# The last 24 key steps of attention in threes, with a third place for scores and six adds on another engine

## The chip, the core and the metric

The program runs on one core of a Trainium2 chip. The core has TensorE (PE in the profile, with its weight loads as PEld), VectorE (DVE), ScalarE (ACT), GpSimd (POOL) and SyncE (SP, which here only starts DMAs). Each engine executes its own instructions in the order in which the program issued them and waits on semaphores for the others. Matmul results go to PSUM, which has room for eight tiles of 128 x 512 float32; everything else lives in SBUF or in DRAM, and sixteen DMA engines move data. The metric is device microseconds from the first to the last instruction of one execution; the time of a kernel is the median over its runs.

## The reference

Two blocks, run twice: attention with 32 heads of 32 columns over 2048 tokens of 1024 columns, and a feed-forward (SwiGLU, 3584 wide) on only the eight tokens that score highest.

```
x = A_x
x = x + A(layernorm(x));  x = x + B(layernorm(x))
x = x + A(layernorm(x));  x = x + B(layernorm(x))

A: q, k, v = split(x @ wqkv);  p = softmax(q k^T / sqrt(32));  return (p v) @ wo
B: r = x @ w_r;  idx = the 8 largest r;  xs = x[idx]
   y = (silu(xs @ w_gate) * (xs @ w_up)) @ w_down;  y = y * sigmoid(r[idx])
   return x with y added in the rows idx
```
All is float32. The kernel multiplies float32 as sums of rounded high and low parts where it needs the precision.

## The kernel before, in words

`layer(n, ...)` is one attention with its feed-forward; layer 1 is a generator whose first stages are interleaved with the end of layer 0, and it takes over layer 0's feed-forward. Scheduling is manual: each engine runs its instructions in program order, and the framework adds the semaphores and hands out buffers of a pool as earlier tiles in them come free.

**Attention.** The work is cut into 32 units: a group of four heads (8 groups) by a block of 512 queries (4 blocks). A unit has 16 key steps of 128 keys. The loop over `s` goes through all 512 steps; for step `s`:

- `scores` (L698) makes two half steps of scores, two heads each, with four matmuls per half into a PSUM tile `pre` of 128 x 1024. There are two such tiles.
- ACT takes the exponential of each half (L1099) into the step's tile `P`, 128 x 2048 float32. There are nine `P` buffers (`PB`).
- `pv_step` (L1025) multiplies an earlier step's `P` by the values into one PSUM tile `pv`; in the last 25 steps it is two steps behind.
- `pre_mm` (L688) multiplies queries and keys once more, 25 steps ahead (`LEAD`), and DVE takes the row maxima of it (L696) from the three PSUM tiles `st`. So in the last 25 steps there is no such work, and DVE is nearly free.
- The denominators: `emit` (by the table `EVENTS`, made by `unit_events`) adds the 16 `P` tiles of a unit into `acc`. Ten tiles are joined in pairs by DMAs that add in SBUF (`merge`, L1038, issued by POOL), and eight adds of 128 x 2048 go to POOL (`acc_add`, L1035, at the steps of `ADDED`). The last unit has no merges: its twelve adds are on DVE. `sum_mm` (L1045) multiplies `acc` and two or three `P` tiles left over by ones on PE, and ACT copies the result (L1055). For the second-to-last unit this comes in step 22, counted from that unit's start.

A `P` buffer is free again when its P times V and its add, merge or sum are done.

PSUM is full: `pre` 2 x 2 places, `pv` 1, `st` 3. After the loop and the last `sum_mm` comes the output projection (L1238), tile by tile of 128 tokens, with the residual, the layer norm's statistics and the router's logits on DVE (L1243 to L1273).

**The end of layer 1.** The last two tiles (L1303) are handled apart: `row_sums` (L1312, L1315), `logits`, `normed`, and between them `first_rows` and `last_rows`, which pick the candidates of the router and gather their rows. Then `finish` runs 49 steps of the feed-forward: for each of two halves eight gate steps, eight up steps (L531, accumulated in the PSUM tile `pv`) and a transpose (L548), then 14 down steps (L563) and the final scatter (L579). The gate's result is made into its silu by ACT (L538, L539), DVE (L540, L541) and POOL (L542), and DVE multiplies it with up (L544). Weights are loaded by SP as buffers come free. In between, `choose` ranks the candidates, and `back(1)` and `back(0)` move rows of the output into their places: each gathers rows (POOL, L216), loads eight rows (ACT's queue, L382) and scatters both (POOL, L220). POOL waits in its queue for each of these transfers before it starts the next that depends on it.

## Time and profile before

| | us |
|---|---|
| median of 3 runs (4557.66 to 4558.62) | 4558.31 |
| the profiled execution | 4557.8 |
| its span, first to last instruction | 4556.0 |
| PE busy in the span | 4506.4 |
| from the scores of step 8 of the second-to-last unit to the output projection, layer 0 | 64.94 |
| the same in layer 1 | 64.97 |
| PE busy in these two stretches | 62.39 and 62.38 |
| from 4440 to the end: length, and PE busy in it | 116.00, 90.89 |

A profile's row gives the time at which a group of like instructions starts (us from the start of the span), its length, engine and line, the operation with the tiles that it writes and reads, the count, and in brackets how long the engine was idle before it and what ended that. Engines that wait often belong to a chain: the view of the chain goes back from the last instruction to whatever released it. A busy PE is not PE at its best, since matmuls overlap and their ends are modelled; waits inside a stretch are better seen in the distance from start to start. Rows of stretches give the busy time of each engine in a window, TensorE's granted clock, the DMA engines' share and GB/s.

### The profile page before, as it was taken

To read this page: it belongs to the slowest core of one execution; us is meant where nothing else is said; L and a number is where in the kernel's file an instruction comes from. 1 tells how busy PE (TensorE), PEld (TensorE's weight loads), DVE (VectorE), ACT (ScalarE), POOL (GpSimd) and SP (SyncE) were. 2 spreads that over 40 slices of the span, in tenths; PEclk is the share of its full clock that TensorE was granted. 3 is DMA by queue.
4 is the path that set the end of the run, shared out by engine and by line. 5 is a ranking of instruction groups with operands and counts; after the bars stand their busy time and mean duration, and the time that the engine had idled before them with its cause. 6 is when DMAs were issued, how large, how long until landed. Compare 5 with 4: busy or idle time off the path is not lost.

```text
span 4556.0 us, 73559 instructions
## 1 busy us (share of the span) xinstructions
PE 4506.4 (99%) x29241; PEld 2686.4 (59%) x29241; DVE 3150.2 (69%) x4963; ACT 2428.5 (53%) x2574; POOL 3231.7 (71%) x1251
## 2 busy tenths in 40 slices
PE   9999999999999999999999999999999999999997
PEld 7888745555555555548877786555555555555583
DVE  2211588888888888876522225888888888888663
ACT  3322267767676767670222222767777676767510
POOL 4444378989898889855633343888989898989452
PEclk9999999999999999999999999999999999999998
DMA  6757477777777768758698774877777777777598
GB/s 206 210 171 207 130 170 154 171 156 160 167 163 158 172 145 180 168 122 242 183 318 279 252 207 122 175 153 166 164 152 174 157 160 167 164 158 175 140 277 322
DMA packets 329719, 833.62 MB, mean 183 GB/s; under 512 B 43996, under 2 KB 160732, under 8 KB 280206
## 3 DMA queue, kind: packets, MB, share of 16 engines
q1 hardware_dynamic: 275454, 476.43, 35.4%
q0 software_dynamic: 45248, 325.67, 35.3%
q10 hardware_dynamic: 8672, 26.81, 2.2%
q8 instruction: 230, 3.77, 0.3%
q14 instruction: 115, 0.94, 0.1%
HBM read 384.34 MB, written 119.47 MB: 111 GB/s over the span
## 4 chain that ended last, share of the span: by engine, by line
PE 94%; DMA 2%; POOL 1%; issue 1%; DVE 1%; ACT 0%; ACTq 0%; POOLq 0%; SPq 0%; DVEq 0%
PE pv L1025 22%; PE pre L703 21%; PE st L821 17%; PE st L688 16%; PE pre L821 6%; PE pre L1238 5%; PE st L1045 4%; POOL acc L1035 1%; PE pv L531 1%; PE pre L688 1%; PE pv L821 0%; PE pre L790 0%; DMA ord<-rd 0%; PE st L571 0%; PE pre L1303 0%
## 5 line engine op out<-in xcount | busy, mean ns | idle before, releaser
L696 DVE TENSOR_REDUCE nm<-st 128x1 f32<-128x512 f32 x3916 | 2434.0, 684 | 376.1 <-PE st L688 370.1
L1099 ACT ACTIVATE P<-pre 128x1024 f32<-128x1024 f32 x2048 | 1985.9, 1022 | 723.3 <-PE pre L703 521.4
L1035 POOL TENSOR_TENSOR acc<-acc,P 128x2048 f32<-128x2048 f32 x434 | 2103.9, 4848 | 86.2 <-DMA P<-P 75.4
L703 PE MATMUL pre<-q,ks 64*128 64x512 f32 (+1 forms) x8192 | 1142.4, 396 | 4.3 <-ACT P L1099 4.3
L1025 PE MATMUL pv<-P,v 128*32 128x512 f32 x8192 | 1092.8, 606 | 4.8 <-DMA v<-vd 4.8
L688 PEld LDWEIGHTS st<-ks,q 64*128 64x128 f32 x3916 | 547.0, 184 | 907.4 <-DVE nm L696 764.9
L688 PE MATMUL st<-ks,q 64*128 64x512 f32 x3916 | 985.9, 471 | 0.5
L703 PEld LDWEIGHTS pre<-q,ks 64*128 64x128 f32 (+1 forms) x8192 | 776.1, 187 | 186.0 <-ACT P L1099 57.4
L1038 POOL DMA_DIRECT2D P<-P x310 | 296.8, 957 | 260.0 <-PE st L688 189.3
L836 DVE TENSOR_TENSOR lo<-st,hi 128x512 fp32r<-128x512 f32 x128 | 88.4, 692 | 528.4 <-ACT hi L835 505.2
L756 POOL TENSOR_TENSOR ohl<-wraw,ord 128x2048 fp32r<-128x2048 f32 (+1 forms) x54 | 222.5, 4124 | 308.1 <-ACT ord L751 299.5
L756 POOL TENSOR_TENSOR wl<-wraw,wh 128x2048 fp32r<-128x2048 f32 (+1 forms) x54 | 222.4, 4122 | 303.7 <-ACT wh L755 284.9
L835 ACT CAST hi<-st 128x512 fp32r<-128x512 f32 x128 | 75.2, 587 | 496.5 <-PE st L821 493.3
L1025 PEld LDWEIGHTS pv<-P,v 128*32 128x32 f32 x8192 | 162.5, 108 | 261.3 <-issue 253.6
L1035 POOL TENSOR_TENSOR acc<-P 128x2048 f32<-128x2048 f32 x62 | 294.0, 4742 | 11.0 <-ACT P L1099 11.0
L1238 PE MATMUL pre<-woh,ohl 128*128 128x512 f32 x960 | 223.2, 390 | 0.0
L1238 PEld LDWEIGHTS pre<-woh,ohl 128*128 128x128 f32 x960 | 180.0, 188 | 39.6 <-ACT ohl L1170 1.7
L821 PE MATMUL st<-xh,wh 128*128 128x512 f32 x512 | 201.4, 393 | 0.0
L821 PE MATMUL st<-xh,wl 128*128 128x512 f32 x512 | 199.6, 390 | 0.0
L821 PE MATMUL st<-xl,wh 128*128 128x512 f32 x512 | 199.5, 390 | 0.0
L151 POOL TENSOR_TENSOR rs<-mv,eps_c 128x1 f32<-128x1 f32 x64 | 29.3, 457 | 232.2 <-DVE mv L149 232.2
L1170 ACT CAST ohl<-ord 128x1024 fp32r<-128x1024 f32 x32 | 33.6, 1052 | 269.9 <-DVE ord L1161 115.7
(384 smaller groups left out, 3995.7 us busy)
## 6 DMA issues: line engine op xcount, KB each, us to landing
P<-P POOLq DMA_DIRECT2D x310, 1024.0 KB, 8.8
wraw<-in_A_wqkv_dram SPq DMA_DIRECT2D x96, 1024.0 KB
q<-qh SPq DMA_DIRECT2D x256, 128.0 KB
ks<-kh SPq DMA_DIRECT2D x112, 256.0 KB
fw<-in_B_w_down_dram SPq DMA_DIRECT2D x17, 1024.0 KB
vd<-vn SPq DMA_DIRECT2D x32, 512.0 KB
qh<-hi SPq DMA_DIRECT2D x64, 256.0 KB
ql<-lo SPq DMA_DIRECT2D x64, 256.0 KB
```

The source lines that it names most:

```text
L688: pe.matmul(ps[b], Q[u][rows, i, 0, qt * 128:(qt + 1) * 128], KS[(u // QC) % 2][rows, i, 0, j * 512:(j + 1) * 512], start=True, stop=True, ...
L696: dve.tensor_reduce(NM[u][:, j, 2 * i + b:2 * i + b + 1, qt], ps[b], axis=AX.X, op=OP.max, negate=True)
L703: pe.matmul(p[:, b * 512:(b + 1) * 512], KS[(u // QC) % 2][rows, i, slot, kt * 128:(kt + 1) * 128], Q[u][rows, i, slot, :], start=(slot == ...
L756: pool.tensor_tensor(wl[:, sl], raw[:, sl], wh[:, sl].bitcast(F32), op=OP.subtract)
L821: pe.matmul(p, *pair(a, l, r), start=(a == 0 and k == 0), stop=(a == KD - 1 and k == 2))
L836: dve.tensor_tensor(lo, p, hi.bitcast(F32), op=OP.subtract)
L1025: pe.matmul(PV[u][32 * h:32 * h + 32, :], V[g][:, kt, 32 * h:32 * h + 32], P[s][:, h, :], start=(kt == 0), stop=(kt == NT - 1), tile_posit ...
L1035: (dve if on_dve else pool).tensor_tensor(o, a, P[u * NT + k].rearrange("p h c -> p (h c)"), op=OP.add)
L1038: pool.dma_start(P[u * NT + a], P[u * NT + b], accum_op=OP.add)
L1045: pe.matmul(p[32 * h:32 * h + 32, :], ones32, a[:, h, :], start=(i == 0), stop=(i == len(parts) - 1), tile_position=(0, 32 * h))
L1099: act.activation(P[s][:, 2 * i:2 * i + 2, :].rearrange("p h c -> p (h c)"), p, AF.Exp, scale=SCALE)
L1238: pe.matmul(p[:, bl], l[:, a, :], r[a][:, bl], start=(k == 0 and a == 0), stop=(k == 2 and a == KD - 1))
```

## The change

It has seven edits.

1. The three `st` places move into a PSUM pool of their own, `banks`. For the last 24 steps it is closed and opened again with one `st` and one `third` tile of 128 x 1024, which is a third place for scores; after the attention it is set back.
2. Those 24 steps run in threes: the six halves of three steps use `pre`, `pre`, `third` in turn. After the third half comes the P times V that is due, with the bookkeeping (`rest_of_step`: the events, DMA issues) of the first step; after the sixth come the next two P times V and the bookkeeping of the other two steps.
3. In the second-to-last unit the six adds of steps 9, 12, 14, 15, 16 and 20 go to DVE. Two adds (steps 5 and 6) and the merges stay on POOL.
4. In layer 1's feed-forward the up product accumulates in an `st` tile, not in `pv`.
5. `back` becomes a generator with a pause between the gather and load and the scatters; `finish` runs the parts after steps 3 and 8 (`back(1)`, before after step 2) and 17 and 25 (`back(0)`, before after step 9).
6. In layer 1's output projection the scaling of the last tile's attention result (`scale_o(NT - 1)`, L1161) moves on DVE from before the normalisation and the logits of tile 12 to behind them.
7. In `row_sums` the statistics of the first half come ahead of the step of `last_rows`, no longer behind it.

```diff
-def unit_events(last):
-    if last:
+ON_DVE = 9
+def unit_events(left):
+    if left == 0:
...
-    ev += [(at, "end", 1, "add", (k, FIRST if at == ADDED[0][0] else None, False)) for at, k in ADDED]
+    ev += [(at, "end", 1, "add", (k, FIRST if at == ADDED[0][0] else None, left == 1 and at >= ON_DVE)) for at, k in ADDED]
...
+    def share_banks(wide):
+        for st, _ in [banks["now"]] if banks else []:
+            st.close()
+        st = ExitStack()
+        banks["now"] = st, st.enter_context(tc.tile_pool(name="banks", bufs=1, space=PSUM))
+        banks["wide"] = wide
...
     def ps_st():
-        return psum.tile([128, 512], F32, name="st", bufs=3)
+        return banks["now"][1].tile([128, 512], F32, name="st", bufs=1 if banks["wide"] else 3)
...
             self.gather(rows, perm["ab"][:, 1:2], self.dst)
             act.dma_start(last, self.dst[end - 8:end, :])
+            yield
             self.scatter(perm["ab"][:, 0:1], rows, self.dst)
             self.scatter(perm["routed"], last, self.dst)
+            yield
...
-                    self.acc = ps_pv()
+                    self.acc = ps_st() if self.n and k == "u" else ps_pv()
...
+            parts = {0: choice, 2: choice, 3: backs[1], 8: backs[1], 17: backs[0], 25: backs[0]}
...
-                if i in (0, 2):
-                    next(choice)
-                if i == 9:
-                    self.back(0)
+                if i in parts:
+                    next(parts[i])
...
-        def scores(u, kt, i):
-            p = ps_pre()
+        def scores(u, kt, i, third=False):
+            p = banks["now"][1].tile([128, 1024], F32, name="third") if third else ps_pre()
...
+            threes = NS - LEAD + 1
+            for s in [*range(threes), *range(threes, NS, 3), *range(NS, NS + 14)]:
+                if threes <= s < NS:
+                    if s == threes:
+                        share_banks(True)
+                    for k in range(6):
+                        half_step(s + k // 2, k % 2, k % 3 == 2)
+                        if k == 2:
+                            pv_step(s - 2)
+                            rest_of_step(s)
+                    for k in (1, 2):
+                        pv_step(s - 2 + k)
+                    for k in (1, 2):
+                        rest_of_step(s + k)
+                    continue
...
-                if n and t == NT - 4:
-                    scale_o(NT - 1)
...
                 dve.scalar_tensor_tensor(waste, xn, 1.0, wrb, op0=OP.mult, op1=OP.mult, accum_out=rcols[:, t:t + 1])
+                if n and t == NT - 4:
+                    scale_o(NT - 1)
...
                     dve.tensor_tensor(o, p[i][h], o, op=OP.add)
+                    dve.bn_stats(st[:, h, :], o)
                     if between and h == 0:
                         next(between)
-                    dve.bn_stats(st[:, h, :], o)
```

More of the change, by code (lines that the diff above doesn't have):

```diff
@@ L599, in finish @@
         def finish(self):
-            choice = self.choose()
+            choice, backs = self.choose(), [self.back(i) for i in range(2)]
+            parts = {0: choice, 2: choice, 3: backs[1], 8: backs[1], 17: backs[0], 25: backs[0]}
             for i in range(len(self.steps)):
@@ L1080, in emit @@
                     if 0 <= v < NU:
-                        todo += [(kt + NT * back, pri, fn, args, v) for (k, pos, pri, fn, args) in EVENTS[v == NU - 1]
+                        todo += [(kt + NT * back, pri, fn, args, v) for (k, pos, pri, fn, args) in EVENTS[min(NU - 1 - v, 2)]
                                  if k == kt + NT * back and pos == where]
@@ L1089, in layer, with half_step, rest_of_step @@
             wop = None
[L1090 removed]
+            def half_step(s, i, third=False):
+                if i == 0:
+                    P[s] = aw.tile([128, 4, 512], F32, name="P", bufs=PB)
+                p = scores(*divmod(s, NT), i, third)
+                act.activation(P[s][:, 2 * i:2 * i + 2, :].rearrange("p h c -> p (h c)"), p, AF.Exp, scale=SCALE)
+            shared = {}
+            def rest_of_step(s):
                 u, kt = divmod(s, NT)
[L1092 to L1093 removed]
                 pr = pre_rows[s + LEAD] if s + LEAD < NS else None
[L1095 to L1104 removed]
                 emit(s, "mid")
@@ L1129, in layer @@
                     f(*args)
+            threes = NS - LEAD + 1
+            assert (NS - threes) % 3 == 0
+            for s in [*range(threes), *range(threes, NS, 3), *range(NS, NS + 14)]:
[12 more added lines that the diff above has]
+                    continue
+                pr = pre_rows[s + LEAD] if s + LEAD < NS else None
+                if pr:
+                    pre_mm(*pr, 0, False)
+                for i in range(2 if s < NS else 0):
+                    half_step(s, i)
+                if pr:
+                    pre_mm(*pr, 1, False)
+                t = s - 1 if s < NS - LEAD else s - 2
+                if s != NS - LEAD and 0 <= t < NS:
+                    pv_step(t)
+                rest_of_step(s)
+            wor, WOR, last_sum = shared["wor"], shared["WOR"], shared["sum"]
         if not prev:
```

36 lines of the change are left out of this document (13 added, 23 removed).

## The prediction

> **What bounds the kernel now.** I read the page's busy line and chain first, then the chain in order of time and the engines' timelines over the attention tail, and then the end of the kernel.
>
> ```profile
> PE 4506.4 (99%) x29241; PEld 2686.4 (59%) x29241; DVE 3150.2 (69%) x4963; ACT 2428.5 (53%) x2574; POOL 3231.7 (71%) x1251
> ...
> L1099 ACT ACTIVATE P<-pre 128x1024 f32<-128x1024 f32 x2048 | 1985.9, 1022 | 723.3 <-PE pre L703 521.4
> ...
> P<-P POOLq DMA_DIRECT2D x310, 1024.0 KB, 8.8
> ```
> ```profile
> 2001.00 6.48 POOL acc L1035
> ...
> 2028.04 2.71 PE pv L1025 x24
> 2030.76 3.43 PE st L1045 x32
> 2034.19 33.27 PE pre L1238 x144
> ...
> 4287.05 153.03 PE pre L1238 x672
> ```
> TensorE is nearly always busy, so only places where it waits can give time back. The second fence (the chain in order of time, both layers) shows one: a POOL add on the chain inside the last 24 key steps. I count key steps from the start of a layer's second-to-last unit, so these are 8 to 31, and T0 is the start of the scores of step 8.
>
> ```profile
> 1957.01 1.10 PE L703 MATMUL pre<-q,ks 64*128 64x512 f32 x8
> 1957.95 0.49 PE L688 MATMUL st<-ks,q 64*128 64x512 f32 x2
> ...
> 1969.25 0.73 PE L703 MATMUL pre<-q,ks 64*128 64x512 f32 x4 [0.69 <-ACT P L1099]
> ...
> 1971.84 1.19 PE L703 MATMUL pre<-q,ks 64*128 64x512 f32 x8
> 1972.96 1.07 PE L1025 MATMUL pv<-P,v 128*32 128x512 f32 x8
> 1973.95 1.45 PE L703 MATMUL pre<-q,ks 64*128 64x512 f32 x8
> ...
> 2002.95 0.74 PE L703 MATMUL pre<-q,ks 64*128 64x512 f32 x4 [0.18 <-ACT P L1099]
> 2003.62 1.07 PE L1025 MATMUL pv<-P,v 128*32 128x512 f32 x8
> ...
> 4222.08 0.74 PE L703 MATMUL pre<-q,ks 64*128 64x512 f32 x4 [0.69 <-ACT P L1099]
> ```
> ```profile
> 1968.18 3.84 ACT L1099 ACTIVATE P<-pre 128x1024 f32<-128x1024 f32 x4
> 1972.67 1.94 ACT L1099 ACTIVATE P<-pre 128x1024 f32<-128x1024 f32 x2 [0.65 <-PE pre L703]
> ...
> 1977.12 1.94 ACT L1099 ACTIVATE P<-pre 128x1024 f32<-128x1024 f32 x2 [0.39 <-PE pre L703]
> ...
> 1981.64 1.94 ACT L1099 ACTIVATE P<-pre 128x1024 f32<-128x1024 f32 x2 [0.44 <-PE pre L703]
> ...
> 2000.96 1.94 ACT L1099 ACTIVATE P<-pre 128x1024 f32<-128x1024 f32 x2 [1.59 <-POOL acc L1035]
> 2007.51 1.94 ACT L1099 ACTIVATE P<-pre 128x1024 f32<-128x1024 f32 x2 [4.61 <-POOL acc L1035]
> ```
> T0 to the output projection is 2034.19 - 1969.25 = 64.9 us in layer 0 and 4287.05 - 4222.08 = 65.0 in layer 1. From these rows: a half step's scores (four matmuls) keep PE 0.47 (1957.01 to 1957.95 is eight), 0.67 ahead of a P times V (2002.95 to 2003.62). P times V costs 1.00 (1972.96 to 1973.95), 0.86 where another follows (2.71 for three). An exponential can start 0.83 after its scores do (1971.84 to 1972.67); exponentials follow each other by 0.94 (3.84 for four), one takes 1.02 (the page), and PE goes on 0.05 after one ends (2000.96 + 1.94 to 2002.95).
>
> With two places for scores, the half steps are tied in a ring over two steps: exponential ends, 0.05, scores 0.67, P times V 1.00, next scores to exponential 0.83, two exponentials 0.94 + 1.02. That is 4.51, or 2.255 a step; the trace has 1981.64 - 1977.12 = 4.52 for two. So neither PE nor ACT is the bound of this stretch: the two places are. Following these numbers row by row through 24 steps, with both POOL waits in place, I get 65.1 for the 64.9 seen; without the POOL waits 62.1.
>
> **The change, part by part.**
>
> *Threes with a third place.* PE's own work in three steps is six halves, 2 x (0.47 + 0.47 + 0.67), and P times V 1.00 + 0.86 + 1.00: 6.08. One wait is left: the sixth half reuses the third place, whose exponential ends at 0.83 + 2 x 0.94 + 1.02 = 3.73 after the first scores, where PE arrives at 3.55; with 0.05 for the handover it waits 0.23. So 6.31 for three, 2.10 a step, and 8 x 6.31 = 50.5 against 24 x 2.255 = 54.1: 3.6 us less in each layer. Then come the denominator of the second-to-last unit inside the stretch (0.86 + 0.86 + 1.00), two more P times V (1.72) and the last denominator (3.43): 50.5 + 2.72 + 1.72 + 3.43 = 58.4. The bookkeeping of the steps comes later in the program, but SP's and POOL's issues keep their order among themselves. The two changes of PSUM pool, and st with one buffer, cost nothing: ACT and DVE have read the old tiles several us before the next writer comes.
>
> *Six adds from POOL to DVE.* The two POOL waits go (62.1 to 65.1: 3.0 us). What is late next is DVE:
>
> ```profile
> 1992.67 3.81 DVE L1035 TENSOR_TENSOR acc<-P 128x2048 f32<-128x2048 f32 x1 [10.30 <-ACT P L1099]
> 1996.58 34.62 DVE L1035 TENSOR_TENSOR acc<-acc,P 128x2048 f32<-128x2048 f32 x11
> ```
> ```profile
> L1035 DVE TENSOR_TENSOR acc<-acc,P x11: 2291/2293/6497, 1996.6 to 2028.9; 128x2048 f32<-128x2048 f32 x11
> ```
> An add took up to 6.50 while POOL was adding, and 2.29 in the median; two slow ones leave (34.62 - 13.0)/9 = 2.40 from start to start. Afterwards POOL has no add left in the stretch, so I take 2.40 (upper end 3.81 to 6.50 if something else slows it). Add 10 needs merge 10, which needs P times V of 10 (ends T0 + 11.9 in the new order) and 8.8 to land: T0 + 20.7. Then add 10 and 13 more queue behind each other (adds of steps 1 to 12 of the last unit, and P 12 between the third and fourth): 20.7 + 14 x 2.40 = 54.3. PE needs the last at 58.4 - 0.98 = 57.4, so DVE has 3.1 us in hand. P 12 is added by T0 + 32.7, before the denominator reaches it (33.4). Counting the P tiles not yet added at each step, at most eight of nine are held, so I give the buffers no wait; the upper end is rival 3.
>
> A rule that speaks against this: the Trainium skill, "SBUF — State Buffer", "Who interferes with whom", has DMAs issued from GpSimd starved of descriptor writes while VectorE holds the shared pair, though it infers that tensor_tensor takes only its read side. No run here shows adds on DVE beside merges. If a merge waited one whole add, 2.3 us, the chain would end at 56.6 and the sum would stay; it needs no more than the 3.1 in hand.
>
> So 64.9 to 58.4: **6.5 us in each layer, 13.0 together**. Between the layers, loads start from buffers that the output projection frees, so I expect the first 6.5 to carry through.
>
> *The end of layer 1.*
>
> ```profile
> 4437.74 1.23 DVE L1161 TENSOR_TENSOR ord<-ord 128x1024 f32<-128x1024 f32 x1 [3.46 <-DMA ord<-rd]
> ...
> 4466.00 0.23 DVE L470 TENSOR_SCALAR ohl<-st,pos 128x8 f32<-128x8 f32 x1 [0.70 <-PE st L468]
> 4466.15 0.68 DVE L1315 BATCH_NORM_STATS2 bst<-x 128x6 f32<-128x512 f32 x1
> ```
> ```profile
> 4441.16 3.88 PE L1303 MATMUL pre<-wol,ohl 128*128 128x512 f32 x16 [1.09 <-ACT ohl L1170]
> ...
> 4489.49 1.93 PE L531 MATMUL pv<-fw,xs 128*32 128x512 f32 x16 [1.19 <-ACT xn L539]
> ...
> 4503.00 1.11 PE L548 MATMUL st<-ident,xn 128*128 128x128 f32 x4 [6.43 <-DVE xn L544]
> ```
> ```profile
> 4518.57 5.14 DMA out_dram<-wrb,first
> ```
> ```profile
> 4500.06 0.86 POOL L220 DMA_INDIRECT out_dram<-wrb,routed  x1 [4.70 <-DMA out_dram<-x,ab]
> ```
> ```profile
> 4500.00:4510.00 10.00, 7.00 (x37) 2.30 (x40) 1.38 (x2) 0.00 (x0) 3.02 (x3) 0.66 1.02 400
> 4520.00:4530.00 10.00, 9.13 (x48) 2.62 (x44) 1.24 (x2) 0.00 (x0) 0.73 (x1) 1.00 1.03 411
> 4530.00:4540.00 10.00, 10.00 (x50) 2.70 (x46) 0.00 (x0) 0.00 (x0) 0.00 (x0) 1.00 1.02 407
> ```
> ```profile
> 4540.00:4542.00 2.00, 2.00 (x12) 0.59 (x10) 0.00 (x0) 0.00 (x0) 0.00 (x0) 1.00 1.02 410
> 4542.00:4544.00 2.00, 2.00 (x12) 0.47 (x9) 0.00 (x0) 0.00 (x0) 0.00 (x0) 1.00 0.48 193
> 4546.00:4548.00 2.00, 0.34 (x2) 0.00 (x0) 0.74 (x1) 0.00 (x0) 0.58 (x1) 1.00 0.00 0
> ```
> The scaling of the last tile waits 3.46 for its DMA with the logits of tile 12 queued behind it on DVE, and those hold the PSUM tile that PE's L1303 wants: moved behind them, PE's 1.09 goes, about 1.0 of it on the path. The statistics ahead of the pick fill its 0.70 wait: 0.6. Both lie on the chain that leads to the routed rows, so the feed-forward starts 1.6 earlier. The gate accumulator no longer has to be read before the up products start (1.19 in the first half), and POOL's multiply no longer stands behind a scatter that waits 4.70 for a scatter, which cost PE most of 6.43. Together over 7 us of PE, but I count little of it: from 4490 on the DMA engines are full (share 1.02, 400 GB/s) with weights, until some way into 4542 to 4544, and PE stops at 4546.3, 2.3 us later. PE may not finish before the last weights and one more half step of the down product, near 4545: 1.0 us. The end gives **1.6 + 1.0 = 2.6**. Each `back` is a gather, an ACT load and two scatters. The first's scatters move from step 2 of the feed-forward to 8, behind the multiply of step 7; the second's gather and load from 9 to 17 and its scatters to 25, behind the second multiply. POOL has nothing else queued behind them, and their last transfer, before at 4518.57, stays a chain of transfers that started 6 us apart, some 20 us ahead of the final scatter. The second's ACT load waits for the first's scatters and can hold the second half's exponential by some 2 us, which the full DMA engines hide as well.
>
> A second rule bears here: PEclk is 0.66 in 4500 to 4510, after the 6.43 us idle. The Trainium skill, "TensorE: Matmul & The Clock Gate", "What's actually happening", has PE fall to half clock after an idle window of about 3.4 us; the trace agrees. By that rule the restart at half clock goes too, which is again hidden by the weights.
>
> **Sum.** 4557.8 (this profiled execution; span 4556.0) - 13.0 - 2.6 = 4542.2; the median of the runs is 0.5 higher, so 4542.7.
>
> **The rivals.**
> 1. The weights are not the floor: PE's 6.43 + 1.19 come back beyond the 1.6: 13.0 + 1.6 + 7.6 gives 4536. Against it: three slices with DMA share over 1.0.
> 2. The third place is worth nothing, because scores of three halves and two P times V in a row wait elsewhere; only the POOL waits go: 2 x 3.0 + 2.6, 4549.7. For it: nothing but that no such order is in the trace.
> 3. The buffer waits move to DVE: step 21's tile waits for the add of P 12 (T0 + 32.7 or a little later). My row-by-row count then gives 63.7, so 1.2 a layer: 4553.3. For it: before, exponentials waited for just such adds (1.59 and 4.61). Against: P 12 is no longer behind 6.5 us adds.
> 4. The other side: DVE's chain of adds ends last. Its place is the 14 adds after T0 + 20.7. It delays PE from 2.62 us an add on, eats the whole gain with the end's 2.6 from 3.18, and is 0.2% slower than before from 3.5. At the 3.81 of the first DVE add the projection starts at 20.7 + 53.3 + 1.0 = 75.0, 10.1 later in each layer: 4576. For it: 3.81 and 6.50 are in the trace. Against: they coincide with POOL adds, which are gone.
>
> **How the numbers follow.** 0.2% of 4558 is 9.1 us, about what a measurement can tell from no change. Forecast, with down to two thirds of its tail gain: 0.69 (faster; own range 4540 to 4547). Rival 1 0.05 (faster). Rival 2 0.07, rival 3 0.07, and 0.03 for a loss elsewhere that leaves under 9 us (same). Rival 4 0.09 (slower). So faster 0.74, same 0.17, slower 0.09. The range 4539 to 4554 leaves out rivals 1 and 4, 0.14.
>
> **What would show it.** Exponentials in the stretch 2.10 apart per step with a wait once in three; no ACT wait for POOL; DVE adds at 2.29 ending some 3 us ahead of the last denominator; T0 to the output projection 58 to 59 in both layers; PE's 6.43 gone, replaced by waits for weights in the down product. The prediction is wrong if DVE adds stretch past 2.6, if exponentials wait for DVE, or if the down product runs without waiting for weights.

## The result, and the profile after

The changed kernel takes 4547.71 us (median of 11 runs, 4543.33 to 4550.17) against 4559.5 for the kernel before (11 runs, 4553.04 to 4561.37): ratio 0.9974, 95% interval 0.9967 to 0.9982, so 11.8 us faster, where 15.6 were predicted: inside the stated range of 4539 to 4554, and 0.7 us above the forecast's own 4540 to 4547. The profiled execution took 4545.36 us with a span of 4543.6, that is 12.4 less span than the profile before.

The page's busy line; PE is busy 8.7 us less than the 4506.4 of before, the rest of the 12.4 is idle time less. The two stretches from T0 to the projection account for the busy time: 57.90 and 57.97 us, for 62.39 and 62.38 before, with the same number of matmuls, which suggests that rows of the old order were drawn out by waits inside them:

```profile
PE 4497.7 (99%) x29241; PEld 2686.0 (59%) x29241; DVE 3156.8 (69%) x4975; ACT 2426.5 (53%) x2574; POOL 3169.1 (70%) x1239
```

Now the tail of layer 0 on PE (the timeline: start, length, line, operation, count, and in brackets the wait ahead of it and what ended it), with the first tile of the output projection of layer 1 as the last two rows; then the exponential between two of its rows on ACT; then the denominator's row of the kernel before:

```profile
1967.74 0.74 PE L721 MATMUL pre<-q,ks 64*128 64x512 f32 x4 [0.69 <-ACT P L1112]
...
1974.26 1.20 PE L721 MATMUL pre<-q,ks 64*128 64x512 f32 x8
...
1977.94 0.74 PE L721 MATMUL third<-q,ks 64*128 64x512 f32 x4
...
1980.47 1.21 PE L721 MATMUL pre<-q,ks 64*128 64x512 f32 x8
...
2002.06 1.06 PE L1063 MATMUL st<-acc,ones 128*32 128x512 f32 x8 [1.15 <-DVE acc L1053]
...
2026.96 3.31 PE L1283 MATMUL pre<-woh,ohl 128*128 128x512 f32 x13
...
2050.19 7.54 PE L1283 MATMUL pre<-woh,ohl 128*128 128x512 f32 x32 [0.85 <-DVE pre L1316]
...
4276.22 0.73 PE L1283 MATMUL pre<-woh,ohl 128*128 128x512 f32 x2 [0.35 <-ACT ohl L1214]
4277.48 5.76 PE L1283 MATMUL pre<-woh,ohl 128*128 128x512 f32 x24 [0.53 <-DVE ohl L1217]
```
```profile
1976.86 1.03 ACT L1112 ACTIVATE P<-third 128x1024 f32<-128x1024 f32 x1
```
```profile
2007.53 1.07 PE L1045 MATMUL st<-acc,ones 128*32 128x512 f32 x8 [1.13 <-POOL acc L1035]
```

Three steps take 1980.47 - 1974.26 = 6.21 us, and no exponential waits for an add. The second use of the third place starts at 1977.94, 0.05 after the exponential of its first use ends (1976.86 + 1.03 = 1977.89), so this place is what holds PE there, as the prediction worked out. T0 to the output projection is 2026.96 - 1967.74 = 59.2 (64.9 before). But four waits of PE are left. One stands where the kernel before had one for POOL: 1.15 in the denominator of the second-to-last unit, now for DVE (1.13 before; in layer 1 it is 0.89, 1.14 before). Three are new: 0.35 and 0.53 in the first tile of layer 1's projection, and 0.85 at the third tile of layer 0's.

The end of layer 1 on PE, two rows of the second half's feed-forward from the kernel before, and two slices of the engines (length, busy time of PE, PEld, DVE, ACT, POOL with counts, PEclk, DMA share, GB/s):

```profile
4429.78 3.79 PE L1348 MATMUL pre<-wol,ohl 128*128 128x512 f32 x16
...
4484.28 0.66 PE L566 MATMUL st<-ident,xn 128*128 128x128 f32 x4 [0.88 <-DVE xn L562]
...
4502.06 0.81 PE L566 MATMUL st<-ident,xn 96*128 96x96 f32 x4 [3.26 <-DVE xn L562]
4502.80 3.29 PE L581 MATMUL st<-ord,ht 128*32 128x512 f32 x8
...
4530.29 3.63 PE L581 MATMUL st<-fw,ht 128*32 128x512 f32 x16 [0.64 <-DMA fw<-in_B_w_down_dram]
```
```profile
4513.70 6.21 PE L531 MATMUL pv<-fw,xs 128*32 128x512 f32 x42 [1.18 <-ACT xn L539]
...
4521.64 0.55 PE L548 MATMUL st<-ident,xn 96*128 96x96 f32 x4 [0.87 <-DVE xn L544]
```
```profile
4520.00:4530.00 10.00, 7.64 (x32) 1.59 (x32) 0.00 (x0) 0.00 (x0) 0.00 (x0) 1.00 1.03 408
4530.00:4532.00 2.00, 1.71 (x8) 0.49 (x10) 0.00 (x0) 0.00 (x0) 0.00 (x0) 1.00 0.62 248
```

The 6.43 is down to 0.88 and the first half's 1.19 is gone. The second half's waits grew from 1.18 + 0.87 to 3.26, so these waits together fell from 9.7 to 4.1 us. From its seventh step on the down product now waits for a weight at nearly every step (seven waits, 4.2 us in all), while the DMA engines are full until the last weights are in.

Starts of PE's rows cut the kernel into stages. "Tail" is T0 to the start of the second tile of the output projection, "end 1" from there in layer 1 to the first product of the last two tiles, "end 2" to the first gate product, "end 3" to the end of PE's last matmul (all in us):

| stage | before | after | difference |
|---|---|---|---|
| start to T0, layer 0 | 1969.25 | 1967.74 | -1.5 |
| tail, layer 0 (of it to the projection) | 76.3 (64.9) | 70.5 (59.2) | -5.8 |
| second tile to T0 of layer 1 | 2176.6 | 2178.6 | +2.0 |
| tail, layer 1 (of it to the projection) | 76.4 (64.9) | 71.4 (59.4) | -4.9 |
| end 1 | 142.7 | 141.5 | -1.2 |
| end 2 | 36.8 | 36.3 | -0.5 |
| end 3 | 68.4 | 67.9 | -0.5 |

In the runs below, which share the first and third stage with one or the other kernel, these two lie between 1967.5 and 1971.3, and (but for one run, which is told of) between 2175.6 and 2177.4. So the -1.5 and the +2.0 (0.85 of it the wait at the third tile) are run to run for the most part, and the change itself is the two tails and the end: -10.7 and -2.2.

### The profile page after: what moved, and what is told of

Read it like the earlier page. It is cut to its first block, busy times and chain, and to the rows that moved or that the text cites. A ratio compares the mean times of both kernels' runs of the same rounds, so it can differ in the third digit from the quotient of the medians.

```text
span 4543.6 us, 73545 instructions
## 1 busy us (share of the span) xinstructions
PE 4497.7 (99%) x29241; PEld 2686.0 (59%) x29241; DVE 3156.8 (69%) x4975; ACT 2426.5 (53%) x2574; POOL 3169.1 (70%) x1239
## 4 chain that ended last, share of the span: by engine, by line
PE 94%; DMA 2%; DVE 2%; issue 1%; POOL 1%; ACT 0%; SPq 0%; ACTq 0%; POOLq 0%; DVEq 0%
PE pv L1043 22%; PE pre L721 21%; PE st L839 17%; PE st L706 16%; PE pre L839 5%; PE pre L1283 5%; PE st L1063 4%; PE pv L549 1%; PE pre L706 1%; PE pv L839 0%; DMA ord<-rd 0%; PE pre L808 0%; DMA wraw<-in_A_wqkv_dram 0%; DVE acc L1053 0%; PE third L721 0%
## 5 line engine op out<-in xcount | busy, mean ns | idle before, releaser
L1112 ACT ACTIVATE P<-pre 128x1024 f32<-128x1024 f32 x2016 | 1955.2, 1022 | 704.2 <-PE pre L721 515.6
L1053 POOL TENSOR_TENSOR acc<-acc,P 128x2048 f32<-128x2048 f32 x422 | 2038.4, 4830 | 84.3 <-DMA P<-P 74.7
L721 PE MATMUL pre<-q,ks 64*128 64x512 f32 (+1 forms) x8064 | 1117.8, 395 | 1.7 <-ACT P L1112 1.7
L721 PEld LDWEIGHTS pre<-q,ks 64*128 64x128 f32 (+1 forms) x8064 | 765.2, 186 | 162.1 <-ACT P L1112 27.0
```

The costliest lines, as they stand in the source:

```text
L721: pe.matmul(p[:, b * 512:(b + 1) * 512], KS[(u // QC) % 2][rows, i, slot, kt * 128:(kt + 1) * 128], Q[u][rows, i, slot, :], start=(slot == ...
L1053: (dve if on_dve else pool).tensor_tensor(o, a, P[u * NT + k].rearrange("p h c -> p (h c)"), op=OP.add)
L1112: act.activation(P[s][:, 2 * i:2 * i + 2, :].rearrange("p h c -> p (h c)"), p, AF.Exp, scale=SCALE)
```

## The experiments

Totals of single runs differ by some us, so I read the stages from each run's profile. Each edit is shown against the changed kernel, the first against the kernel before.

| kernel | profiled us | tail, layer 0 (to the projection) | tail, layer 1 (to the projection) | ends 1, 2, 3 |
|---|---|---|---|---|
| adds_alone | 4549.93 | 72.9 (61.6) | 74.1 (62.0) | 142.5, 36.8, 68.1 |
| threes_alone | 4555.25 | 76.8 (64.7) | 76.8 (64.7) | 141.5, 36.3, 67.1 |
| p12_early | 4542.0 | 70.5 (58.5) | 70.3 (58.2) | 142.9, 36.3, 67.2 |
| last_15_first | 4543.62 | 70.5 (59.2) | 70.2 (58.9) | 141.5, 36.3, 68.2 |
| p12_15_merge | 4550.47 | 69.6 (57.8) | 70.6 (58.5) | 142.0, 36.7, 68.6 |
| second_in_x | 4542.99 | 70.5 (59.2) | 70.1 (58.9) | 141.5, 36.9, 67.7 |
| all_four | 4539.03 | 69.1 (57.7) | 69.0 (57.7) | 141.5, 36.2, 66.9 |
| fewer_weights | 4541.05 | 70.5 (59.2) | 71.5 (59.4) | 141.5, 36.2, 62.9 |
| feed_undone | 4549.09 | 70.5 (59.2) | 71.4 (59.4) | 142.6, 36.5, 68.9 |
| rows_undone | 4546.53 | 70.5 (59.2) | 71.3 (59.3) | 143.5, 36.8, 68.3 |

(End 1 holds a wait at an earlier tile than the last two in some runs: 1.16 at the third in p12_early, 0.44 at the third in adds_alone, 0.64 and 0.27 at later ones in feed_undone and p12_15_merge.)

**1. The adds alone** (the old order stays).

```diff
-    ev += [(at, "end", 1, "add", (k, FIRST if at == ADDED[0][0] else None, False)) for at, k in ADDED]
+    ev += [(at, "end", 1, "add", (k, FIRST if at == ADDED[0][0] else None, left == 1 and at >= ON_DVE)) for at, k in ADDED]
```

> The kernel before with only the six adds of the second-to-last unit moved to DVE; the old order with two places for scores stays. T0 is the start of the scores of step 8 of the second-to-last unit; T0 to the output projection was 64.9 before and is 59.2 with the whole change in layer 0. Theory (two separate limits, the ring of two places and the POOL waits): both POOL waits of the exponentials (1.59 and 4.61) go, the ring stays at 4.5 for two steps, the stretch is 62.1 to 62.5 in both layers. Rival 1 (the adds are only a means for the threes and give nothing alone): 64.9. Rival 2 (the exponentials wait for DVE's adds instead): 63.5 to 64.5 with waits for acc from DVE in ACT's rows.

T0 to the projection is 61.6 and 62.0; the ring goes on and no exponential waits for an add. ACT's timeline, layer 0:

```profile
1975.36 1.94 ACT L1103 ACTIVATE P<-pre 128x1024 f32<-128x1024 f32 x2 [0.37 <-PE pre L707]
...
1979.80 1.94 ACT L1103 ACTIVATE P<-pre 128x1024 f32<-128x1024 f32 x2 [0.37 <-PE pre L707]
```

Two steps take 1979.80 - 1975.36 = 4.44. The theory's mechanism holds and both rivals fall, though both layers lie 0.1 to 0.5 under its 62.1 to 62.5: the adds give 3.3 and 2.9 of the 5.7 and 5.5 that the way from T0 to the projection got shorter.

Timed in rounds:

> The kernel adds_alone timed in rounds. Its profile has 3.3 and 2.9 us less in the two tails and 0.8 and 0.6 more at the third tiles. Theory: 5 to 7 us below the kernel before, ratio 0.9984 to 0.999, about half of what the whole change gave. Rival (the single time, 7.1 us below, was chance): within 3 us of the kernel before.

4551.49 us (11 runs, 4549.17 to 4553.63) against 4557.43 for the kernel before: 5.9 us less, ratio 0.9988, interval 0.9979 to 0.9997. About half of the change's gain, as its stages say.

**2. The threes alone** (with the edits of the end).

```diff
-ON_DVE = 9
+ON_DVE = 99
```

> The whole change but for the adds: all eight adds of the second-to-last unit stay on POOL. Theory (two limits in one stretch, the later one counts): POOL was busy without a break until T0 + 38.3 before, so the last buffer wait still ends there; the 26.7 us that follow get shorter by 0.15 us for each of some ten steps. The stretch is 63 to 63.7, so that the threes alone give 1 to 2 of the 5.7 us that the change gave in layer 0. Rival 1 (the third place is worth its 3.6 by itself): 61.3. Rival 2 (nothing, POOL sets the end): 64.9.

64.7 in both layers, above the theory's 63 to 63.7. The theory missed and rival 2 holds: the threes alone give next to nothing. ACT's, POOL's and DVE's timelines, layer 0:

```profile
2001.62 1.02 ACT L1112 ACTIVATE P<-third 128x1024 f32<-128x1024 f32 x1 [0.94 <-POOL acc L1053]
...
2008.17 1.02 ACT L1112 ACTIVATE P<-pre 128x1024 f32<-128x1024 f32 x1 [4.61 <-POOL acc L1053]
```
```profile
1989.67 18.47 POOL L1053 TENSOR_TENSOR acc<-acc,P 128x2048 f32<-128x2048 f32 x3
```
```profile
1991.65 5.51 DVE L1053 TENSOR_TENSOR acc<-P 128x2048 f32<-128x2048 f32 x1 [7.00 <-ACT P L1112]
```

The last wait for POOL ends 2008.17 - 1969.44 (T0 in this run) = 38.7 after T0, against 38.3 before. What the faster order wins ahead of it is waited away there. Behind it 26.0 are left, against 26.6 before: of the 1.5 that the theory had, 0.6 came. Another 0.55 is a wait of PE at the first tile, because ACT's first cast of the projection stood 1.29 for the scaling of `ord`, which stands behind the adds on DVE. The rows also show why POOL is so slow: its adds take 18.47 / 3 = 6.2, and DVE's first one beside them 5.51, where it took 2.28 in the run of the adds alone. Taken one by one, the adds of this run end in turn: POOL at 1995.00, DVE at 1997.16, POOL at 2001.59, DVE at 2003.73, POOL at 2008.14, so a DVE add ends 2.1 to 2.2 after POOL's and a POOL add 4.4 after DVE's. So each seems to wait for the other's to end, and the two engines take turns. The Trainium skill, "SBUF — State Buffer", "Who interferes with whom", says that a VectorE instruction with two SBUF inputs contends with a GpSimd instruction that reads SBUF; these rows agree.

**3. P 12 added earlier.** In the changed kernel PE's new 1.15 ends with the add of P 12. DVE, POOL and the merges (joined by DMAs that POOL issues) of the changed kernel in layer 0, and as the last line the time from issue to landing of these four merges (least, median, most):

```profile
1979.33 2.29 DVE L1053 TENSOR_TENSOR acc<-acc,P 128x2048 f32<-128x2048 f32 x1 [9.61 <-DMA P<-P]
1985.61 2.29 DVE L1053 TENSOR_TENSOR acc<-acc,P 128x2048 f32<-128x2048 f32 x1 [3.98 <-DMA P<-P]
...
1990.51 2.29 DVE L1053 TENSOR_TENSOR acc<-acc,P 128x2048 f32<-128x2048 f32 x1 [0.95 <-DMA P<-P]
1992.72 2.28 DVE L1053 TENSOR_TENSOR acc<-P 128x2048 f32<-128x2048 f32 x1
1995.11 28.27 DVE L1053 TENSOR_TENSOR acc<-acc,P 128x2048 f32<-128x2048 f32 x12
2023.30 1.22 DVE L1205 TENSOR_TENSOR ord<-ord 128x1024 f32<-128x1024 f32 x1
```
```profile
1971.45 0.88 POOL L1056 DMA_DIRECT2D P<-P  x1 [6.38 <-ACT P L1112]
1974.91 0.86 POOL L1056 DMA_DIRECT2D P<-P  x1 [2.58 <-ACT P L1112]
1980.25 0.86 POOL L1056 DMA_DIRECT2D P<-P  x1 [4.48 <-ACT P L1112]
1983.72 0.86 POOL L1056 DMA_DIRECT2D P<-P  x1 [2.60 <-ACT P L1112]
```
```profile
DMA to landing us min/median/max: 7.8/10.4/11.7
```

The second and third merge are issued 5.34 apart and DVE's adds of them start 4.90 apart; the first two are issued 3.46 apart and the adds start 6.28 apart. The first of the four needs 7.8, the others 10.1 to 11.7. The spacing goes with this: in the same stretch of layer 0, merges issued 5.1 to 5.3 behind another took 8.3 to 8.6 in the kernel before and 9.0 to 9.4 in threes_alone, those 4.4 to 4.5 behind another 9.4 to 10.5 in adds_alone. DVE's adds beside them are hardly the reason: a single merge issued while DVE was adding took 7.0 and 7.9 us in the two layers of experiment 5, 8.1 and 7.9 in experiment 7. So closer together than some 5 us they seem to queue, about 5 us each. Merge 10 was issued at T0 + 12.5 and its add could start at T0 + 22.8, and the add of P 12 is fifth on DVE from there (the third of the twelve in one row): 1995.11 + 2 x 2.36 + 2.29 = 2002.1, where PE's wait ends (2002.06).

```diff
-    ev += [(at, "end", 1, "add", ...) for at, k in ADDED]
+    ev += [(18 if left == 1 and k == 12 else at, "end", 1, "add", ...) for at, k in ADDED]
```

> The whole change, with the add of P 12 of the second-to-last unit emitted at step 18 in place of 20, so that it is third on DVE behind merge 10 and not fifth. With the change PE waits 1.15 in the middle denominator for that add, which ended at T0 + 34.3. Theory: the add of P 12 waits for its merge, which landed at T0 + 27.6, and ends near T0 + 30; PE's 1.15 goes in both layers, T0 to the output projection goes from 59.2 to 58.1 in layer 0 and from 59.4 to 58.3 in layer 1; the last of DVE's adds still ends at T0 + 55.6. Rival 1: PE's wait is only the first of several and the time comes back as waits of the exponentials or at the last denominator: 59.0. Rival 2: DVE's chain is delayed by the wait for the merge and the last denominator waits for it: 59.5 or more.

PE's 1.15 goes, and T0 to the projection is 58.5 and 58.2. But in layer 0 the first tile gives it back, 70.5 to the second tile as without it. In layer 1, whose first tile waited already (see 4), 71.4 becomes 70.3. PE, ACT and DVE in that run, layer 0:

```profile
2000.63 1.04 PE L1063 MATMUL st<-acc,ones 128*32 128x512 f32 x8
...
2026.11 0.73 PE L1283 MATMUL pre<-woh,ohl 128*128 128x512 f32 x2 [0.67 <-ACT ohl L1214]
```
```profile
2025.02 1.04 ACT L1214 CAST ohl<-ord 128x1024 fp32r<-128x1024 f32 x1 [1.40 <-DVE ord L1205]
```
```profile
1995.39 28.46 DVE L1053 TENSOR_TENSOR acc<-acc,P 128x2048 f32<-128x2048 f32 x12 [0.46 <-DMA P<-P]
```

DVE's adds end at 56.2 after T0, 0.6 later than in the changed kernel. So DVE's chain is the next limit, though not at the last denominator, as rival 2 had it: behind the adds stands the scaling of the first tile, which ACT's cast and PE wait for.

**4. The order of the last denominator.** In layer 1 of the changed kernel the cast of the first tile waits for PE:

```profile
4275.12 1.04 ACT L1214 CAST ohl<-ord 128x1024 fp32r<-128x1024 f32 x1 [1.09 <-PE st L1063]
```

```diff
-LAST_DIRECT = (13, 14, 15)
+LAST_DIRECT = (15, 14, 13)
```

> The whole change, with the three P tiles of the last denominator multiplied in the order 15, 14, 13 in place of 13, 14, 15. With the change the first cast of ohl in layer 1 waits 1.09 for the last denominator, and PE waits 0.35 and 0.53 in the first tile of the output projection; before and in layer 0 this wait is not there. Theory (the ohl tile lies on the place of P 15, whose product comes third): the cast starts 0.9 earlier, both waits of PE go, T0 to the second tile of the projection goes from 71.4 to 70.5 in layer 1 and stays at 70.5 in layer 0. Rival 1 (the ohl tile lies on P 13 or on two of the tiles): no change or less than 0.5. Rival 2 (the cast waits for something else that ends then): no change.

As the theory has it: the cast starts without a wait, the projection runs through from 4274.88, T0 to the second tile goes from 71.4 to 70.2 in layer 1 (0.9 of it the two waits), and layer 0 stays. PE's timeline, layer 1:

```profile
4274.88 7.69 PE L1283 MATMUL pre<-woh,ohl 128*128 128x512 f32 x32
```

The adds alone have the waits of 0.35 and 0.54 in layer 1 too, the kernel before doesn't, though pools and tiles are the same: which place of the nine a P tile gets changes with the order in which places come free. That P 15 then lay under `ohl` is what this run points to; the addresses themselves I did not follow.

**5. One DVE add less.** Added to 3 and 4:

```diff
-        return [(k + 1, "mid", 1, "add", ...) for k in range(1, NT) if k not in LAST_DIRECT]
+        ev = [(k + 1, "mid", 1, "add", ...) for k in range(1, NT) if k not in LAST_DIRECT + (8, 9)]
+        return ev + [(10, "end", 0, "merge", (8, 9)), (13, "mid", 0, "add", (8, None, True))]
```

> The whole change with P 12 added at step 18, the order 15, 14, 13 in the last denominator, and one of the last unit's twelve DVE adds replaced by a merge (P 9 into P 8, issued at step 10, added at step 13 ahead of P 12). With P 12 early alone, DVE's chain ended at the same time as before (T0 + 56.1), the scaling of the first tile behind it on DVE came 1.4 late for ACT's cast, and PE lost 0.67 and 0.52 in the first tile: T0 to the second tile was 70.5 in layer 0 as without it. Theory (DVE's chain of adds is the next limit, 2.3 us later than it may end): with one add less the scaling comes 2.3 earlier, both of PE's waits go, and T0 to the second tile is 69.2 to 69.5 in both layers, 2.2 to 2.4 us less in all than with the order of the last denominator alone (70.5, 70.2). Rival 1 (the cast then waits for the end of the last denominator or for ACT): 70.0 to 70.5. Rival 2 (the merged tile lands late or holds a buffer, exponentials or the last denominator wait): 70.5 or more.

A miss in two ways. First, the tails are 69.6 and 70.6, not 69.2 to 69.5: by the mechanism of rival 2, DVE stood for the merge, so its chain ended hardly earlier. The merge itself was quick (7.0 and 7.9 us), but it was issued only 43.5 after T0 (the two rows of DVE are layer 0 and 1):

```profile
2019.25 4.69 DVE L1054 TENSOR_TENSOR acc<-acc,P 128x2048 f32<-128x2048 f32 x2 [1.55 <-DMA P<-P]
...
4272.57 4.69 DVE L1054 TENSOR_TENSOR acc<-acc,P 128x2048 f32<-128x2048 f32 x2 [2.75 <-DMA P<-P]
```

Second, the run lost 6 us between the layers (2182.8 where the others have 2175.6 to 2177.4), nearly all at the third tile of layer 0's projection. PE, and the slice of the engines:

```profile
2051.99 10.41 PE L1284 MATMUL pre<-woh,ohl 128*128 128x512 f32 x32 [2.68 <-DVE pre L1317]
```
```profile
2050.00:2060.00 10.00, 8.01 (x23) 6.40 (x24) 9.19 (x11) 1.04 (x1) 7.13 (x8) 0.66 0.83 226
```

It is the wait that was 0.85 in the changed kernel, here 2.68, and behind it the tile took 10.41 where it takes 7.54 else, with a granted clock of 0.66 in the slice. DVE frees `pre` late because the first tile's `xn` waits for `rd<-xn`: the last denominators, on their way through DRAM, lie in `xn`. Here DVE first stood 3.02 for the transfer `ord<-rd`, with the reciprocal of these denominators queued behind it, and then 1.43 for `rd<-xn`. In the changed kernel the wait for `rd<-xn` alone was 2.75. Why the transfers of this run were later than the others' stays open.

**6. The last denominators out of `xn`** (with 4).

```diff
-            second = XN[:, 0:256]
+            second = rest[:, 512:768]
```

> The whole change with the order 15, 14, 13 in the last denominator, and with the second half's denominators (second, 128 x 256) loaded into a free part of the tile rest, no longer into xn. With the change the first tile's xn waits on DVE for the transfer rd<-xn (2.75 in layer 0, 1.5 to 2.7 elsewhere), and in some of the stretches PE then waits for the PSUM tile that DVE frees behind it (0.85 at the third tile of layer 0; 1.16 and, at half clock behind it, 2.68 in other runs; none in others). Theory (the shared tile xn is the cause): DVE's xn of the first tile no longer waits for rd<-xn, PE has no wait above 0.1 at the third tile in either layer, and the third tile starts 10.9 after the second in both. Rival (DVE is late for another reason, the statistics or POOL): the wait of xn stays above 1 with another releaser, and PE's wait can come back.

DVE's first `xn` no longer waits for the transfer, and the third tile starts 10.9 after the second in both layers. The first is the evidence, since three of nine profiles with the adds on DVE and the old place have no wait of PE there either:

```profile
2047.02 0.81 DVE L1314 TENSOR_SCALAR xn<-x,mv,rs 128x1024 f32<-128x1024 f32 x1 [0.72 <-POOL rs L169]
```

**7. All four together**, with the merge one step earlier.

```diff
-        ev = [(k + 1, "mid", 1, "add", ...) for k in range(1, NT) if k not in LAST_DIRECT + (8, 9)]
-        return ev + [(10, "end", 0, "merge", (8, 9)), (13, "mid", 0, "add", (8, None, True))]
+        ev = [(k + 1, "mid", 1, "add", ...) for k in range(1, NT) if k not in LAST_DIRECT + (7, 8)]
+        return ev + [(9, "end", 0, "merge", (7, 8)), (13, "mid", 0, "add", (7, None, True))]
```

> As the run before, and P 12 added at step 18, and one of the last unit's twelve DVE adds replaced by a merge of P 8 into P 7, issued at step 9, added at step 13 ahead of P 12. The merge of P 9 into P 8 at step 10 was issued only at T0 + 43.5, landed at T0 + 50.5, and DVE stood 1.55 and 2.75 for it. Theory (DVE's chain with that wait is what PE's first tile waits for): a merge one step earlier is issued 3 us sooner, lands before DVE reaches it, the chain ends some 2 us earlier, and T0 to the second tile is 69.0 to 69.4 in both layers (70.5 and 70.2 with the order of the last denominator alone, 69.55 and 70.58 with the later merge). The profiled time is 4539 to 4541, 4 to 6 below the change's. Rival 1 (the merge lands too late again): 69.5 to 70.6 with a wait of DVE for P<-P ahead of the last two adds. Rival 2 (the tail is limited by ACT's casts and the last denominator): 69.8 or more, without a wait of DVE.

> The kernel all_four timed in rounds. By the stages of its profile it is some 6 us below the changed kernel (1.4 and 2.4 in the two tails, 1.1 and 0 at the third tiles, 1 at the end), of which the stages that the edits touch give 4 to 5 and the rest is run to run. Theory: ratio to the kernel before 0.996 to 0.9965, that is 16 to 18 us, against 11.8 (0.9974) of the change. Rival (the profile was a lucky run): ratio 0.997 or more, no difference from the change.

T0 to the second tile is 69.1 and 69.0, and PE has no wait in the first tiles. PE's two projections and DVE's chain in layer 0:

```profile
2026.87 7.68 PE L1284 MATMUL pre<-woh,ohl 128*128 128x512 f32 x32
...
4271.52 7.68 PE L1284 MATMUL pre<-woh,ohl 128*128 128x512 f32 x32
```
```profile
1996.85 25.99 DVE L1054 TENSOR_TENSOR acc<-acc,P 128x2048 f32<-128x2048 f32 x11 [0.46 <-DMA P<-P]
2022.76 1.22 DVE L1206 TENSOR_TENSOR ord<-ord 128x1024 f32<-128x1024 f32 x1
```

DVE's chain ends 53.6 after T0 (2022.76 - 1969.13), 1.9 earlier than in the changed kernel (55.6). Timed, 4541.45 us (5 runs, 4538.9 to 4542.97) against 4557.43: ratio 0.9966, interval 0.9952 to 0.998, 16.0 us less than before. That is between the theory (0.996 to 0.9965) and its rival (0.997 or more), and the intervals of this ratio and the change's overlap, so the totals alone don't part the two; the stages do, by 1.4 and 2.4 in the tails of the single run's profile, and the same again in the timed one's profile (69.1, 69.1).

**8. The end: fewer weights.**

```diff
+            if self.n and k == "d" and a in (1, 2):
+                self.W[u] = self.W0
+                return
...
             self.W[u] = t = place.tile([128, 2048], F32, name=name, bufs=bufs)
+            self.W0 = t
```

> The whole change, but the second and third of the 14 weight tiles of layer 1's down product (1 MB each) are not loaded; their steps multiply with the first tile instead, so the output is not the reference's. PE does as much work as before. Theory (the weights' DMA sets the end): 2 MB at the 410 GB/s of the DMA rows are 5.1 us, PE has 4.2 us of waits for weights in the down product to give back, and the way from the first gate product to PE's last matmul goes from 67.9 (67.1 to 68.2 in four runs) to 63 to 64.5. Rival (PE's own chain, with its restart after 3.26 us of idling, sets the end): 67 to 68.

End 3 is 62.9, 5.0 less for 2 MB, just past the theory's 63 to 64.5 on the far side from the rival: the DMAs of the weights set the end. PE's down product then runs almost without a wait, although its idle of 3.05 ahead of the transpose is still there (PE's timeline):

```profile
4502.50 0.72 PE L570 MATMUL st<-ident,xn 96*128 96x96 f32 x4 [3.05 <-DVE xn L566]
...
4516.67 7.03 PE L585 MATMUL st<-woh,ht 128*32 128x512 f32 x32
...
4525.98 3.63 PE L585 MATMUL st<-fw,ht 128*32 128x512 f32 x16 [0.56 <-DMA fw<-in_B_w_down_dram]
```

**9. The end: edits 4 and 5 undone, and edits 6 and 7 undone.**

```diff
-                    self.acc = ps_st() if self.n and k == "u" else ps_pv()
+                    self.acc = ps_pv()
...
-            parts = {0: choice, 2: choice, 3: backs[1], 8: backs[1], 17: backs[0], 25: backs[0]}
+            parts = {0: [choice], 2: [choice, backs[1], backs[1]], 9: [backs[0], backs[0]]}
...
-                if i in parts:
-                    next(parts[i])
+                for part in parts.get(i, ()):
+                    next(part)
```

> The whole change, but the up product accumulates in pv again and back runs whole after steps 2 and 9, as before (edits 4 and 5 undone). PE's waits of about 1.2 and 6.4 in the feed-forward come back. Theory (the weights set the end, these edits hardly count): from the first gate product to PE's last matmul 67.5 to 68.6, at most 1 us more than with them (67.1 to 68.2 in four runs). Rival (the waits are on the path): 70 or more.

PE's waits are back in full (1.19 and 6.82 in the first half, 1.18 and 0.87 in the second), and end 3 is 68.9, 0.3 above the theory's range and far below the rival's 70:

```profile
4493.27 1.12 PE L566 MATMUL st<-ident,xn 128*128 128x128 f32 x4 [6.82 <-DVE xn L562]
```

The four profiles without these edits (before, the adds alone twice, this one) have 68.4, 68.1, 69.0 and 68.9, mean 68.6; the nine with them and all the weights 66.9 to 68.6, mean 67.7; the two sets overlap at their edges. So the 5.9 us by which edits 4 and 5 shorten PE's waits (10.1 to 4.1) are worth about 0.9.

```diff
                 if low:
                     low()
+                if n and t == NT - 4:
+                    scale_o(NT - 1)
...
-                if n and t == NT - 4:
-                    scale_o(NT - 1)
...
-                    dve.bn_stats(st[:, h, :], o)
                     if between and h == 0:
                         next(between)
+                    dve.bn_stats(st[:, h, :], o)
```

> The whole change, but scale_o of the last tile is ahead of the logits of tile 12 again, and the statistics stand behind the pick (edits 6 and 7 undone). Theory (each is on the path): PE's wait ahead of the last two tiles comes back, the way from the second tile of layer 1's projection to the last two tiles goes from 141.5 to 142.7, and from there to the first gate product from 36.27 to 36.8. Rival (run to run noise): 141.5 and 36.3.

End 1 is 143.5, 0.8 more than the theory had, and end 2 is 36.8; PE waits 1.63 ahead of the last two tiles, where DVE's scaling waits 4.17 for its transfer (PE, then DVE):

```profile
4430.02 3.89 PE L1348 MATMUL pre<-wol,ohl 128*128 128x512 f32 x16 [1.63 <-DVE pre L1318]
```
```profile
4426.60 1.23 DVE L1205 TENSOR_TENSOR ord<-ord 128x1024 f32<-128x1024 f32 x1 [4.17 <-DMA ord<-rd]
```

Without edit 6, end 1 was 142.7, 142.5, 141.5 and 143.5 in four profiles; 141.5 is thirteen tiles without a wait. The last of the thirteen distances, which edit 6 touches, was 12.1, 10.9, 10.9 and 12.7 in them, as that transfer landed, and 10.9 to 11.0 in all ten profiles with edit 6; the rest of the 142.5 stems from earlier tiles. Without edit 7, end 2 was 36.8 to 36.9 in these four; with it, it was 36.2 to 36.9 in ten, six of them 36.2 to 36.3.

## Why the prediction was right, and where it was off

- **The ring of two places and the POOL waits.** The recurrence gave 62.1 for the adds without the threes; 61.6 and 62.0 were measured. That the exponentials' waits go and nothing on DVE takes their place for the exponentials (rival 3) held.
- **The threes.** 6.31 for three steps was forecast, 6.21 measured, with the wait for the third place where it was worked out; 58.4 for the stretch, and 58.5 and 58.2 once P 12 is early. So rival 2 falls for the two edits together. But the working put 3.6 on the threes and 3.0 on the adds as separate terms. They aren't: adds alone 3.3 and 2.9, threes alone 0.2, both 5.7. While POOL's last add sets a point in time at T0 + 38, what is won ahead of it is lost there.
- **P 12 by T0 + 32.7, the denominator at 33.4: this step failed**, with 1.15 and 0.89 of PE's time in the two layers, so that T0 to the projection is 59.2 and 59.4 and not 58 to 59. The term that was mis-sized is the merge's 8.8 from issue to landing, the page's median over 310 merges that took 6.9 to 14.6. Here four were issued 3.5, 5.3 and 3.5 apart, where the same stretch of before has 5.1 to 5.2, and the add of merge 10, which waited for it, started 10.3 after the issue (1990.51 - 1980.25); the merge was also issued 0.6 later than worked out. That the spacing is the cause is likely but rests on few merges (experiment 3). The rule that the prediction set against itself, DVE's adds holding the merges up, is not borne out: the single merges of experiments 5 and 7 took 7.0 to 8.1 us beside such adds, and the kernel before, too, had one (issued at 1988.03, 8.6 us), which the prediction overlooked. The add of P 12, fifth in DVE's queue, ended at T0 + 34.3.
- **DVE's 3.1 us in hand.** DVE's chain was sized well (2.36 from start to start against 2.40) and ended at T0 + 55.6 against 54.3, ahead of the last denominator. The step overlooked what stands behind the adds on DVE: the scaling of the first tile (1.22), which ACT's cast takes up 0.9 ahead of the last denominator. Counted from there DVE has 0.6 in hand (2024.5 to the cast at 2025.09), not 3.1. Rival 4 didn't come: adds stayed at 2.29. Its place was well chosen, since with P 12 early PE's next wait stands behind this chain.
- **Edits that were costed at nothing.** The two PSUM pools did cost nothing: PE's wait ahead of T0 is 0.69 as before, and layer 0's projection starts without one. That the adds' move also moves P tiles to other places, and that one of them then seems to lie under the next phase's `ohl`, was not seen: waits of 0.9 in layer 1.
- **The first 6.5 carries through.** It does, with a reserve: from the second tile on the stages between the layers are the same (2176.6 before; 2175.6 to 2177.4 in the runs with a shorter tail, one apart), but the third tile can come late behind `rd<-xn`: by 0.6 to 2.8 us in one layer or both of six of the nine profiles that have the adds on DVE and the last denominators in `xn`, not in the other three. The kernel before and threes_alone don't show it; whether the adds' move brings it is open.
- **The end**, forecast 1.0 + 0.6 + 1.0: measured 1.2, 0.5 and 0.5 in the profile; over the runs about 0.8 for edit 6 (from 0 to 1.8, as its transfer lands), 0.4 and 0.9. Weights are the floor, as the fewer weights show; rival 1 falls. The restart at half clock, which the prediction took to be gone, moved behind the second half's wait: 4502.80 has eight matmuls of 3.29 for 1.91, after 3.26 of idling.

The sum: 15.6 forecast, less 1.15 + 0.89 for P 12 and 0.9 for `ohl`, is 12.7. The tails and the end gave 12.9: without these waits T0 to the projection would be 58.1 in both layers, 0.3 shorter than forecast in each, and the end gave 0.3 less. The two stages of the run to run parts took 0.5 back, which leaves the 12.4 of the two spans. So the number came out with two errors against the forecast that were not foreseen, and small ones for it; the mechanism of the rest is as forecast.

## What to carry to other kernels

Two limits in one stretch aren't two terms of a sum: the one that sets a fixed point in time hides the other, so ask of each edit what it gives alone. When work moves onto a nearly idle engine, size the slack against everything queued behind it, here the next phase's first instruction, and not only against the consumer you had in mind. A median time to landing over a whole run is no price for four transfers in a row; take it from the nearest rows with the same spacing, and where an order issues transfers of one queue closer together, count them one behind another.

## What the runs showed of the hardware

- A merge of 1 MB, accumulated in SBUF by a DMA that POOL issues, took 7.8 us as the first of four and up to 11.7 behind others, one landing 4.9 to 6.3 after the other (changed kernel, layer 0). The Trainium skill, "DMA: Bandwidth & Descriptors", "Anatomy of one DMA — SWDGE (gpsimd) path", fits a transfer issued by GpSimd with 2.0 us and the bytes over 436 GB/s, which would be an estimate of 4.4 us here; for these transfers, which add, even the first has nearly twice that.
- PE's clock: an idle of 0.85 left the next 32 matmuls at 7.54 (changed kernel), an idle of 2.68 made them 10.41 (experiment 5, granted clock 0.66 over those 10 us), though that is shorter than the window of about 3.4 us that the prediction went by, and after 3.26 the first eight of the down product took 3.29 where later ones take 1.91 (granted clock 0.57 from 4502 to 4506).
- Adds of 128 x 2048 on DVE and POOL at the same time take turns (experiment 2): 5.51 for 2.28 on DVE, 6.2 on POOL, where the page of the changed kernel has 4.83 in the mean.
